# Warming matmuls, 16-bit transposes and their copies in the head of a linear attention and GeGLU kernel

## The chip, the cores and the metric

The kernel runs on one core of one Trainium2 chip. The metric is the device time of one execution in microseconds (us). The core has five engines that run side by side: TensorE (PE) for matmuls and its weight loads (PEld), VectorE (DVE), ScalarE (ACT), GpSimd (POOL) and SyncE (SP), which here only issues DMAs. Matmul results land in PSUM, which the kernel holds as one tile of eight banks of 512 f32 on each of 128 partitions (`ps_all`); DVE and ACT read them from there.

## What is computed

The reference normalises x (2048 tokens, 576 features), and adds to x a linear attention of 32 heads of 18 features and a gated feed-forward network of width 4608, both of the normalised x. Cut to what matters:

```python
xn = _layernorm(x, axis=-1)
return x + _A_ref(xn, A_wqkv, A_wo) + _B_ref(xn, B_w_gate, B_w_up, B_w_down)

def _A_ref(x, wqkv, wo):
    q, k, v = heads(x @ wqkv)
    phi = lambda t: jnp.where(t > 0, t + 1, jnp.exp(t)) + 1e-6
    kv = jnp.einsum("bhsd,bhse->bhde", phi(k), v)
    z = jnp.einsum("bhsd->bhd", phi(k))
    o = einsum(phi(q), kv) / (einsum(phi(q), z) + 1e-6)
    return o @ wo

def _B_ref(x, w_gate, w_up, w_down):
    return (_gelu(x @ w_gate) * (x @ w_up)) @ w_down
```

Inputs and output are bfloat16.

## The kernel before

**Tiles.** The 2048 tokens are 16 tiles of 128. The 576 features are cut into five chunks of contraction: four of 128 and one of 64. The last chunk is doubled: x is held 640 wide (`XW`), with a copy of the last 64 features at its end (the "twin", `x_twin`, on POOL), so that both halves of the array have something to contract. A matmul with `xn` needs it transposed, features on partitions: `xnT`, 128 x 5 x 2048.

**Pairs of row tiles.** Most matmuls use 64 of the array's 128 rows, two at a time, one on the lower (`LO`) and one on the upper (`HI`) half. A `_Unit` (L241) is such work on two PSUM banks. Its first phase, p1, runs five pairs (one per chunk), its second phase, p2, four pairs with the halves swapped between the banks; between the two POOL passes a semaphore on (the "turn", L263). All of these matmuls carry line L252. Units are K and Q (a token tile's keys or queries, 64x288 a matmul) and g (a block of the feed-forward network's gate and up products for 512 tokens, 64x512 a matmul).

**The stages.** The head runs up to about 15 us: it loads x and the first weights, normalises tiles 0 to 3 and transposes them on PE. Then come g0 to g13 (gate and up for the first 512 tokens, kept raw), mixed with K4 to K15, Q2 and Q3 (to 59 us). Tiles 4 to 15 are transposed by a DMA (`dma_transposes`, L352, issued by SP). Then follow the products of keys with xn (L566), and for each 512 tokens the remaining gate and up blocks and the down projection (L855) with the attention's output added in the same banks.

**A tile of the head, 0 to 3.** `ln_half` twice and `ln_aggr` on DVE give mean and variance; `ln_rstd` on ACT gives the reciprocal deviation by a logarithm and an exponential; `ln_norm` on DVE writes xn, in two instructions of 384 and 256 columns. `transposes` (L336) is a matmul with xn as the weights and a 64x64 identity as the moving operand, for each of the two halves of tokens and each chunk, in f32: lower half into bank 0, upper half into bank 1. Its part 0 does three chunks, part 1 two. `tp_copy` (L344, the instructions carry L347) copies part 0 of both banks with ACT and part 1 of both banks with DVE into `xnT`.

**Fillers.** `spin(NWARM)` (L227, L238) runs 35 matmuls of 128x128 zeros at the start, before any data is there, and `row_spin(5)` runs ten small ones after tile 0's transposes.

**The order.** On every engine, instructions run in the order in which they are issued. For PE that order is written out by hand (L448): t0, K0, t1, K0's second phase, K1, Q0, t2, Q1, t3, K2, K3, g0, g1 and so on, a second phase following the next unit's first. `t` stands for the transposes of a tile. For the other engines a small planner decides (`in_order`, L67): each step has an engine, a cost, a rank, predecessors and a time before which it is not due; the planner takes steps by when they can begin and, within 0.05 us, by rank. Its costs and due times (`X_AT`, `W_AT`) fix the order alone.

**Banks.** In the head K0 and Q1 use banks 4 and 5, K1 and K2 banks 6 and 7, Q0 and K3 banks 2 and 3. A unit may begin when the one before it on its banks has been copied out: for K0, Q0, K1, Q1 and K3 by a plain ACT copy (`raw`, L415), for the others through the exponential (`exp`, L420, on ACT) and two DVE steps (`clamp`, L423, and `phi`, L429). So K2 waits for K1's raw copy and K3 for Q0's. g0 and g1 use block 0 of gate and up weights, g2 and g3 block 1, g4 and g5 block 2; each block is loaded as `wr` (the last 64 features, both), `wg` and `wu` (L180 to L184).

**Loads.** SP issues, in this order, tile 0 of x, the key weights, tile 2, the query weights' main part, tile 3, the query weights' last rows, tiles 4 to 7, block 0, tiles 8 and 9, block 1, tiles 10 and 11; then it comes to the DMA transpose of tile 4, which waits for that tile's normalise, and then to block 2. Tile 1 of x is issued by ACT.

Of the kernel before, what the change touches and what calls it, by code (L numbers as in the profile page):

```python
# [8 lines left out]
ACT = mybir.ActivationFunctionType  # L9
ALU = mybir.AluOpType  # L10
BF16 = mybir.dt.bfloat16
# [3 lines left out]
P = 128  # L15
HP = 64
# [11 lines left out]
KT = 5  # L28
# [6 lines left out]
GUB = 2  # L35
NB = NF // GUB
NWBUF = 4
NWARM = 35
XW = D + HP
RAW = 14  # L40
PK0 = 18
# [45 lines left out]
def kernel(  # L87
# [11 lines left out]
    nc = tc.nc  # L99
# [14 lines left out]
    ps_all = psum.tile([P, 8, 512], F32, name="ps_all")  # L114
# [10 lines left out]
    x_sb = persist.tile([P, NS, XW], BF16, name="x_sb")  # L125
    xnT = persist.tile([P, KT, S], BF16, name="xnT")
# [4 lines left out]
    mv = persist.tile([P, NS, nc.vector.BN_AGGR_DIM], F32, name="mv")  # L131
    rstd = persist.tile([P, NS], F32, name="rstd")
    nbias = persist.tile([P, NS], F32, name="nbias")
# [18 lines left out]
    xn = apool.tile([P, NS, XW], BF16, name="xn")  # L152
# [33 lines left out]
    def load_wd(dst, f0, f1, at):  # L186
# [24 lines left out]
    ident = const.tile([P, P], BF16, name="ident")  # L211
# [7 lines left out]
        out=bm3, in_=bm3, compare_op=ALU.is_ge, fill=0.0, base=0, pattern=[[-DH, 7], [0, DH]], channel_multiplier=1,  # L219
    )  # L220
    nc.gpsimd.affine_select(
        out=bm3, in_=bm3, compare_op=ALU.is_ge, fill=0.0, base=DH - 1, pattern=[[DH, 7], [0, DH]], channel_multiplier=-1,
# [4 lines left out]
    def spin(count):  # L227

        for _ in range(count):
            nc.tensor.matmul(ps_all[:, 7, 0:P], lhsT=warm[:], rhs=warm[:], start=True, stop=True)  # L230
# [6 lines left out]

    spin(NWARM)  # L238

# [55 lines left out]
    def step(name, engine, took, rank, after, call, ready=0.0, tail=0.0):  # L295
        steps[name] = _Step(engine, took, rank, after, call, ready, tail)
# [3 lines left out]
    def ln_half(n, h):  # L300
        if n not in ln_raw:
            ln_raw[n] = asmall.tile([P, 2, nc.vector.BN_STATS_DIM], F32, name="stats")
        nc.vector.bn_stats(out=ln_raw[n][:, h, :], in_=x_sb[:, n, h * HALF:(h + 1) * HALF])  # L303

    def ln_aggr(n):
        nc.vector.bn_aggr(out=mv[:, n, :], in_=ln_raw[n][:])
# [8 lines left out]
            out=nbias[:, n:n + 1], in0=mv[:, n, 0:1], scalar1=rstd[:, n:n + 1], scalar2=-1.0, op0=ALU.mult, op1=ALU.mult,  # L315
        )

    def ln_norm(n, c0=0, c1=XW):
        if NORM[n] == "A":
            nc.scalar.activation(  # L320
                out=xn[:, n, c0:c1], in_=x_sb[:, n, c0:c1], func=ACT.Identity, bias=nbias[:, n:n + 1], scale=rstd[:, n:n + 1],
            )
        else:
            nc.vector.tensor_scalar(
                out=xn[:, n, c0:c1], in0=x_sb[:, n, c0:c1], scalar1=mv[:, n, 0:1], scalar2=rstd[:, n:n + 1],
                op0=ALU.subtract, op1=ALU.mult,
            )

    def x_twin(n, cnt):
        nc.gpsimd.tensor_copy(out=x_sb[:, n:n + cnt, D:XW], in_=x_sb[:, n:n + cnt, XW - P:D])  # L330

    HEAD = 4
    TP_CUT = 3
    TP_PARTS = ((0, TP_CUT), (TP_CUT, KT))

    def transposes(n, i):  # L336
        for kt in range(*TP_PARTS[i]):
            for b, rows in enumerate((LO, HI)):
                nc.tensor.matmul(  # L339
                    ps_all[:, b, kt * HP:(kt + 1) * HP], lhsT=xn[rows, n, kt * P:(kt + 1) * P], rhs=ident[rows, rows],  # L340
                    start=True, stop=True, skip_group_check=True,
                )

    def tp_copy(n, i):  # L344
        k0, k1 = TP_PARTS[i]
        copy = nc.vector.tensor_copy if i else nc.scalar.copy
        copy(  # L347
            out=xnT[:, k0:k1, n * P:(n + 1) * P].rearrange("p k (b t) -> p b k t", b=2),
            in_=ps_all[:, 0:2, k0 * HP:k1 * HP].rearrange("p b (k t) -> p b k t", t=HP),
        )  # L350

    def dma_transposes(n):  # L352
        nc.sync.dma_start_transpose(xnT[:, :, n * P:(n + 1) * P], xn[:, n, :])

    X_AT = [3.35, 4.40, 6.90, 9.20]
    W_AT = {"K": 6.00, "Q": 8.80}
    DMA_FREE = 12.7

# [9 lines left out]
    for n in range(NS):  # L368
        first = 1.5 * n if n < 4 else 9.0 + 3.0 * (n - 4)
        both = n // 2 * 2  # L370
        after_x = [("x", both)] if n >= 4 else []
        x_at = X_AT[n] if n < 4 else 11.5 if n < 8 else 2.1 * both
        if n < 4:
            step(("twin", n), "POOL", 0.2, first, [], lambda n=n: x_twin(n, 1), ready=x_at)
        elif n == both:
            step(("twin", n), "POOL", 0.25, first, after_x, lambda n=n: x_twin(n, 2), ready=2.6 * n)
        twin = ("twin", n if n < 4 else both)
        for h in range(2):
            step(("stats", n, h), "DVE", 0.42, first, after_x, lambda n=n, h=h: ln_half(n, h), ready=x_at)
        step(("aggr", n), "DVE", 0.16, first, [("stats", n, 0), ("stats", n, 1)], lambda n=n: ln_aggr(n), tail=0.05)  # L380
        if n < 6:
            step(("rstd", n), "ACT", 0.46, first - 2.0 * (n == 3), [("aggr", n)], lambda n=n: ln_rstd(n, 1))
        elif n == both:
            step(("rstd", n), "ACT", 0.46, first, [("aggr", n), ("aggr", n + 1)], lambda n=n: ln_rstd(n, 2))
        ready = [("rstd", n if n < 6 else both), twin]
        if NORM[n] == "A":
            step(("bias", n), "POOL", 0.27, first, ready[:1], lambda n=n: ln_bias(n))
            ready.append(("bias", n))
        on, took = ("ACT", 0.92) if NORM[n] == "A" else ("DVE", 0.45)
        if n < HEAD:  # L390
            for i, (k0, k1) in enumerate(((0, TP_CUT), (TP_CUT, KT))):
                c0, c1 = k0 * P, k1 * P
                step(("norm", n, i), on, took * (c1 - c0) / XW + 0.05, first, ready, lambda n=n, c0=c0, c1=c1: ln_norm(n, c0, c1), tail=0.05)
                step(("tp", n, i), "PE", 0.05 * (k1 - k0), 0, [("norm", n, i)] + ([("xnT", n - 1, i)] if n else []), lambda n=n, i=i: transposes(n, i), tail=0.15)
                eng = "DVE" if i else "ACT"
                step(("xnT", n, i), eng, 0.26 if i else 0.48, first, [("tp", n, i)], lambda n=n, i=i: tp_copy(n, i), tail=0.02)
            steps[("xnT", n)] = _Step("none", 0.0, first, [("xnT", n, 0), ("xnT", n, 1)], lambda: None, 0.0, 0.0)
        else:
            step(("norm", n), on, took, first, ready, lambda n=n: ln_norm(n), tail=0.05)
            load(("xnT", n), 1.25, 80, first + 2, [("norm", n)], lambda n=n: dma_transposes(n))  # L400
# [59 lines left out]
    def pe(name, took, after, call, ready=0.0):  # L460
        if name in steps:
            s = steps[name]
            s.after = s.after + ([pe_prev[0]] if pe_prev[0] else [])
        else:
            step(name, "PE", took, 0, after + ([pe_prev[0]] if pe_prev[0] else []), call, ready=ready, tail=0.17)
        pe_prev[0] = name
# [27 lines left out]
    for name in line:  # L494
        if name == ".":
            p2_step(pending.pop(0))
            continue
        kind, n = name[0], int(name[1:])
        if kind == "t":
            for i in range(2):  # L500
                pe(("tp", n, i), 0, [], None)
            if n == 0:
                pe("spin", 0.27, [], lambda: row_spin(5))
            continue
        u = _Chain()
        u.name, u.at = name, clock
        if kind in "KQ":
            u.body = _Token(kind, n, head_banks if name in HEAD_T else banks)
            b = u.body.banks
            after = [("xnT", n)]  # L510
            t1, u.t2 = 0.615, 0.49
            u.p1 = u.body.unit.rows
            u.swap = u.body.unit.swap
            u.unit_p2 = u.body.unit.p2
            at = W_AT[kind]
        else:
            u.body = _Raw(n)
            b = u.body.two
            blk = n // GUB
            after = [("xnT", m) for m in range(TPC)] + ([("gu", blk, i) for i in range(2)] if blk else [])  # L520
            t1, u.t2 = 1.08, 0.865
            u.p1 = u.body.rows
            u.swap = lambda body=u.body: body.unit.swap()
            u.unit_p2 = lambda body=u.body: body.unit.p2()
            at = 0.0 if blk else 9.1
        after += owner.get(tuple(b), [])
        pe(("p1", name), t1, after, u.p1, ready=at)
        step(("turn", name), "POOL", 0.06, clock, [("p1", name)], u.swap, tail=0.05)
        clock += t1 + u.t2
        pending.append(u)  # L530
        if len(pending) == 2:
            p2_step(pending.pop(0))
# [407 lines left out]
```

## Time and profile before

| what | value |
|---|---|
| median of three runs | 510.71 us (510.64 to 511.32) |
| the profiled execution's own time | 510.73 us |
| its span, first to last instruction | 509.0 us |
| PE busy | 503.8 us (99%), 4764 matmuls |
| DVE busy | 229.3 us (45%) |
| ACT busy | 152.2 us (30%) |
| POOL busy | 8.2 us (2%) |
| share of PE in the chain that ended last | 95% |
| chain, L252 alone | 59% of the span |
| first real matmul (tile 0's transposes) | 5.57 us |
| g0's first matmul | 15.93 us |
| raw copy of 128x576 on ACT (L415) | 0.63 us |
| normalise on DVE, 384, 256 and 640 columns | 0.37, 0.34, 0.44 us |
| transposes' copy, 384 columns on ACT, 256 on DVE | 0.48, 0.42 us |

Times are read from one profiled execution; the time around the span (510.73 less 509.0) is what the execution takes before its first and after its last instruction. A line of a timeline has start, length, engine, source line, operation, tile written and tiles read, shape, how many instructions are put together, and in brackets the engine's idle time before it and what ended that. A line of the chain that ended last has start, length and what was being done. A busy PE is not PE at its full rate: matmuls overlap, and the length of one includes what it spends in the pipeline. The profile counts a weight load (PEld) by itself.

### The profile page before, as it was taken

The page shows a single profiled execution, that of the slowest core. Times are in us where ns is not written, and L with a number is a line of the kernel's source. Part 1 is how long each engine was busy: PE and PEld are TensorE (multiplying, and loading weights), DVE is VectorE, ACT ScalarE, POOL GpSimd, SP SyncE. Part 2 cuts the span into 40 slices and gives each one's busy share as a digit, 9 for nine tenths or more (in the row PEclk, how much of TensorE's full clock was granted, in tenths as well). Part 3 has the DMA queues.
Part 4 walks back from the last instruction along what each step waited for, and adds up shares of the span by engine and source line. Part 5 has one row for each costly group of instructions (what it writes and reads, how often), then busy time and mean ns, then how long its engine had stood idle before and what let it go on. Part 6 is the DMA issues. An engine that isn't in the chain of part 4 may idle for free.

```text
span 509.0 us, 11185 instructions
## 1 busy us (share of the span) xinstructions
PE 503.8 (99%) x4764; PEld 305.5 (60%) x4764; DVE 229.3 (45%) x481; ACT 152.2 (30%) x265; POOL 8.2 (2%) x32
## 2 busy tenths in 40 slices
PE   8999999999999999999999999999999999999997
PEld 6666775445777544445777444445777444445774
DVE  5777966764101655544101655544101665544101
ACT  3888544335000433223000433233000532232000
POOL 2110000000000000000000000000000000000000
PEclk9999999999999999999999999999999999999999
DMA  9899905996200455663000455663000455640000
GB/s 262 201 229 237 295 3 157 263 259 137 71 13 13 140 152 159 168 180 107 13 13 20 140 158 148 170 175 107 12 13 25 143 152 151 175 116 14 13 12 24
DMA packets 113611, 61.58 MB, mean 121 GB/s; under 512 B 23250, under 2 KB 113562, under 8 KB 113562
## 3 DMA queue, kind: packets, MB, share of 16 engines
q1 hardware_dynamic: 113418, 60.72, 45.1%
q8 instruction: 37, 0.61, 0.5%
q10 hardware_dynamic: 144, 0.15, 0.1%
q14 instruction: 12, 0.10, 0.1%
HBM read 53.75 MB, written 2.36 MB: 110 GB/s over the span
## 4 chain that ended last, share of the span: by engine, by line
PE 95%; DVE 3%; DMA 1%; ACT 0%; issue 0%; DVEq 0%
PE ps_all L252 59%; PE ps_all L855 28%; PE ps_all L566 3%; PE ps_all L860 3%; DVE hT L429 1%; DVE z_sum L537 1%; DMA x_sb<-in_A_x_dram 1%; DVE phi_e L423 0%; PE ps_all L843 0%; PE ps_all L574 0%; DVE stats L303 0%; DVE pq L429 0%; PE ps_all L593 0%; PE ps_all L339 0%; PE ps_all L795 0%
## 5 line engine op out<-in xcount | busy, mean ns | idle before, releaser
L252 PE MATMUL ps_all<-xnT,wg 64*128 64x512 bf16 x1152 | 273.9, 376 | 0.0
L252 PE MATMUL ps_all<-xnT,wu 64*128 64x512 bf16 x1152 | 273.3, 376 | 0.0
L252 PEld LDWEIGHTS <-wg 64*128 64x128 bf16 x1152 | 108.3, 94 | 66.7
L252 PEld LDWEIGHTS <-wu 64*128 64x128 bf16 x1152 | 108.3, 94 | 65.2
L748 DVE TENSOR_TENSOR hT<-ps_all,gl 128x512 bf16<-128x512 f32 x130 | 89.8, 691 | 104.3 <-ACT gl L747 104.1
L855 PEld LDWEIGHTS <-hT 128*128 128x128 bf16 x1152 | 110.8, 98 | 30.9 <-issue 1.3
L747 ACT ACTIVATE gl<-ps_all 128x512 f32<-128x512 f32 x130 | 77.6, 597 | 164.1 <-PE ps_all L252 163.7
L869 DVE TENSOR_TENSOR res<-ps_all,x_sb 128x288 bf16<-128x288 f32 (+2 forms) x32 | 13.8, 454 | 146.3 <-PE ps_all L860 88.1
L855 PE MATMUL ps_all<-wd_a,hT 128*128 128x288 bf16 (+2 forms) x512 | 68.3, 286 | 0.0
L252 PE MATMUL ps_all<-xnT,wr 64*128 64x512 bf16 x288 | 54.9, 376 | 0.0
L855 PE MATMUL ps_all<-hT 128*128 128x288 bf16 (+2 forms) x384 | 52.4, 286 | 0.0
L769 ACT ACTIVATE gl<-ps_all 128x288 f32<-128x288 f32 x24 | 9.2, 409 | 121.4 <-PE ps_all L252 118.9
L855 PE MATMUL ps_all<-wd_m,hT 128*128 128x288 bf16 (+2 forms) x256 | 36.7, 286 | 0.0
L252 PEld LDWEIGHTS <-xnT 64*128 64x128 bf16 x576 | 30.8, 96 | 9.3 <-issue 1.0
L252 PE MATMUL ps_all<-wqkv_sb,xnT 64*128 64x288 bf16 x360 | 27.1, 295 | 0.5 <-ACT hT L415 0.2
L252 PEld LDWEIGHTS <-wr 64*128 64x128 bf16 x288 | 14.2, 94 | 16.3
L860 PE MATMUL ps_all<-m_sb,pqT 128*128 128x288 bf16 (+2 forms) x128 | 20.9, 286 | 0.0
L566 PE MATMUL ps_all<-hT,xn 128*128 128x288 bf16 x128 | 16.0, 286 | 0.0
L444 ACT CAST hT<-ps_all 128x1024 bf16<-128x1024 f32 x14 | 14.1, 1010 | 3.4 <-PE ps_all L252 3.2
L566 PEld LDWEIGHTS <-xn 128*128 128x128 bf16 x128 | 12.4, 98 | 3.5 <-issue 0.5
L860 PEld LDWEIGHTS <-pqT 128*128 128x128 bf16 x128 | 12.4, 98 | 3.3
L303 DVE BATCH_NORM_STATS2 stats<-x_sb 128x6 f32<-128x288 bf16 x32 | 12.8, 432 | 2.6 <-DMA x_sb<-in_A_x_dram 2.6
(79 smaller groups left out, 229.1 us busy)
## 6 DMA issues: line engine op xcount, KB each, us to landing
wg<-in_B_w_gate_dram SPq DMA_DIRECT2D x72, 256.0 KB, 3.0
wu<-in_B_w_up_dram SPq DMA_DIRECT2D x72, 256.0 KB, 3.6
wr<-in_B_w_gate_dram SPq DMA_DIRECT2D x36, 64.0 KB, 3.3
wr<-in_B_w_up_dram SPq DMA_DIRECT2D x36, 64.0 KB, 2.9
wd_a<-in_B_w_down_dram SPq DMA_DIRECT2D x4, 576.0 KB, 7.7
out_dram<-res SPq DMA_DIRECT2D x15, 144.0 KB, 1.8
wqkv_sb<-in_A_wqkv_dram SPq DMA_DIRECT2D x3, 576.0 KB, 5.2
x_sb<-in_A_x_dram SPq DMA_DIRECT2D x6, 288.0 KB, 4.0
```

The costliest lines, as they stand in the source:

```text
L252: return nc.tensor.matmul(self.outs[i], lhsT=self.lhs(i, rows, kt), rhs=self.rhs(i, rows, kt), start=start, stop=stop, skip_group_check=True,)
L303: nc.vector.bn_stats(out=ln_raw[n][:, h, :], in_=x_sb[:, n, h * HALF:(h + 1) * HALF])
L429: nc.vector.scalar_tensor_tensor(out=dst[:, self.n, :].rearrange("p (h c) -> p h c", h=2), in0=self.acc, scalar=0.0, in1=self.e[:].rearran ...
L444: nc.scalar.copy(out=hT[:, self.f:self.f + NF + 1:NF, :], in_=ps_all[:, self.two[0]:self.two[0] + 2, :],)
L537: nc.vector.tensor_tensor(out=(z_bf if i == NS - 1 else z_sum)[:], in0=pk[:, z_order[0], :] if i == 1 else z_sum[:], in1=pk[:, z_order[i], :],
L566: nc.tensor.matmul(ps_all[:, two[hf], :HALF], lhsT=xn[:, n, kt * P:(kt + 1) * P], rhs=pk[:, n, hf * HALF:(hf + 1) * HALF], start=(n == 0), ...
L747: nc.scalar.activation(out=gl[:], in_=ps_all[:, b[0], :], func=ACT.Gelu_apprx_tanh)
L748: nc.vector.tensor_tensor(out=hT[:, GUB * k + i, :], in0=ps_all[:, b[1], :], in1=gl[:], op=ALU.mult)
L769: nc.scalar.activation(out=e[:, :HALF], in_=acc, func=ACT.Exp)
L855: nc.tensor.matmul(self.acc(hf), lhsT=hT[:, f, j * P:(j + 1) * P], rhs=wd(f)[:, self.parts[hf]], start=(f == 0 and not paired), stop=False ...
L860: nc.tensor.matmul(self.acc(hf), lhsT=pqT[:, c, self.ts], rhs=m_sb[:, c, self.parts[hf]], start=False, stop=(paired and c == 3), skip_grou ...
L869: nc.vector.tensor_tensor(out=self.res[:, hs], in0=self.acc(hf), in1=x_sb[:, self.n, hs], op=ALU.add)
```

## The change

Five edits, all in the head.

1. `NWARM` goes from 35 to 43.
2. `ln_norm` always normalises the whole 640 columns of a tile in one instruction, in the head too.
3. `transposes` uses TensorE's transpose with a 16-bit result in place of a matmul with an f32 result, and does all five chunks in one step. The lower token half still goes to bank 0 and the upper to bank 1, now seen as bfloat16.
4. `tp_copy` copies one bank, all five chunks of one token half: ACT takes bank 0, DVE bank 1.
5. In the planner's table a head tile has one normalise and one transposing step; the transposes of a tile wait for both copies of the tile before; costs and two due times are set anew (tile 2 of x at 7.10, the second half of tile 1's statistics at 5.1).

```diff
-NWARM = 35
+NWARM = 43
...
-    def ln_norm(n, c0=0, c1=XW):
+    def ln_norm(n):
...
             nc.vector.tensor_scalar(
-                out=xn[:, n, c0:c1], in0=x_sb[:, n, c0:c1], scalar1=mv[:, n, 0:1], scalar2=rstd[:, n:n + 1],
+                out=xn[:, n, :], in0=x_sb[:, n, :], scalar1=mv[:, n, 0:1], scalar2=rstd[:, n:n + 1],
                 op0=ALU.subtract, op1=ALU.mult,
             )
...
-    TP_CUT = 3
-    TP_PARTS = ((0, TP_CUT), (TP_CUT, KT))
-
-    def transposes(n, i):
-        for kt in range(*TP_PARTS[i]):
+    def tp_bank(b):
+        return ps_all[:, b, :].bitcast(BF16).rearrange("p (k t) -> p k t", t=HP)
+
+    def transposes(n):
+        for kt in range(KT):
             for b, rows in enumerate((LO, HI)):
-                nc.tensor.matmul(
-                    ps_all[:, b, kt * HP:(kt + 1) * HP], lhsT=xn[rows, n, kt * P:(kt + 1) * P], rhs=ident[rows, rows],
-                    start=True, stop=True, skip_group_check=True,
-                )
-
-    def tp_copy(n, i):
-        k0, k1 = TP_PARTS[i]
-        copy = nc.vector.tensor_copy if i else nc.scalar.copy
-        copy(
-            out=xnT[:, k0:k1, n * P:(n + 1) * P].rearrange("p k (b t) -> p b k t", b=2),
-            in_=ps_all[:, 0:2, k0 * HP:k1 * HP].rearrange("p b (k t) -> p b k t", t=HP),
-        )
+                nc.tensor.transpose(tp_bank(b)[:, kt, :], xn[rows, n, kt * P:(kt + 1) * P], ident[rows, rows])
+
+    def tp_copy(n, b):
+        copy = nc.vector.tensor_copy if b else nc.scalar.copy
+        t0 = n * P + b * HP
+        copy(out=xnT[:, :, t0:t0 + HP], in_=tp_bank(b)[:, 0:KT, :])
...
-    X_AT = [3.35, 4.40, 6.90, 9.20]
+    X_AT = [3.35, 4.40, 7.10, 9.20]
...
-            step(("stats", n, h), "DVE", 0.42, first, after_x, lambda n=n, h=h: ln_half(n, h), ready=x_at)
+            step(("stats", n, h), "DVE", 0.42, first, after_x, lambda n=n, h=h: ln_half(n, h), ready=5.1 if (n, h) == (1, 1) else x_at)
...
-            for i, (k0, k1) in enumerate(((0, TP_CUT), (TP_CUT, KT))):
-                c0, c1 = k0 * P, k1 * P
-                step(("norm", n, i), on, took * (c1 - c0) / XW + 0.05, first, ready, lambda n=n, c0=c0, c1=c1: ln_norm(n, c0, c1), tail=0.05)
-                step(("tp", n, i), "PE", 0.05 * (k1 - k0), 0, [("norm", n, i)] + ([("xnT", n - 1, i)] if n else []), lambda n=n, i=i: transposes(n, i), tail=0.15)
-                eng = "DVE" if i else "ACT"
-                step(("xnT", n, i), eng, 0.26 if i else 0.48, first, [("tp", n, i)], lambda n=n, i=i: tp_copy(n, i), tail=0.02)
+            step(("norm", n), on, took, first, ready, lambda n=n: ln_norm(n), tail=0.05)
+            free = [("xnT", n - 1, i) for i in range(2)] if n else []
+            step(("tp", n), "PE", 0.2, 0, [("norm", n)] + free, lambda n=n: transposes(n), tail=0.15)
+            for i, copied in enumerate((0.44, 0.30)):
+                step(("xnT", n, i), "DVE" if i else "ACT", copied, first, [("tp", n)], lambda n=n, i=i: tp_copy(n, i), tail=0.02)
```

## The prediction

> **What bounds the kernel now.** I read the page first: TensorE (PE) is busy in nearly every slice, and the chain that ended last is 95% PE. So time can only be won where PE waits or runs below its rate. Listing who waited for whom, PE has four waits in the whole span: 1.1 us before the first warming matmul, 0.6 at the first transpose, 0.2 at L252 near 13.4, 0.2 near 56.5. Three lie in the first 15 us. The second view is therefore the chain in order of time:
>
> ```profile
> 13.30 0.43 DVE xnT L347
> 13.74 0.02 issue
> 13.76 0.48 ACT xnT L347
> 14.24 0.55 ACT pq L415
> 14.79 0.04 issue
> 14.83 26.96 PE ps_all L252 x306
> ```
>
> The two copies of tile 3's transposes run one after the other, then ScalarE (ACT) copies Q0 out of PSUM, and only that frees the banks of K3, which starts at 14.83. From there PE runs without a hole to 56.25. So a microsecond won ahead of g0 (its first matmul starts at 15.93) is won at the end, if the data for g0 and what follows comes as much earlier. I go by the head alone. The third view is PE's timeline from 4.5 us:
>
> ```profile
> 5.57 0.55 PE L339 MATMUL ps_all<-ident,xn 64*128 64x64 bf16 x10 [0.60 <-DVE xn L324]
> 6.68 1.38 PE L252 MATMUL ps_all<-wqkv_sb,xnT 64*128 64x288 bf16 x10
> ```
>
> The warming matmuls issue every 107 ns from 1.14 to 4.66, then PE stands idle for 0.60 us. Of L252 I then asked two stretches, 8.9 to 10.1 and 11.7 to 12.6 us:
>
> ```profile
> L252 PE MATMUL ps_all<-wqkv_sb,xnT x12: 444/444/444, 8.7 to 9.9; 64*128 64x288 bf16 x12
> L252 PE MATMUL ps_all<-wqkv_sb,xnT x16: 282/283/283, 11.7 to 12.5; 64*128 64x288 bf16 x16
> ```
>
> The same matmul takes 444 ns early and 283 ns later; pair to pair it steps by 240 and 122 ns. PE runs at half its rate until 10.5 us, where the trace's clock record begins at full rate (the clock column reads 1.00 before it too, for want of a record). The 3.9 us of matmuls from 1.05 to 4.97 did not turn the clock; 4.95 us after the work resumed at 5.57 it turned.
>
> **The copies.** Each transposed tile goes ACT first, then VectorE (DVE), or the other way round:
>
> ```profile
> 8.89 0.42 DVE L347 CAST xnT<-ps_all 128x256 bf16<-128x256 f32 x1 [0.53 <-ACT xnT L347]
> 12.34 0.48 ACT L347 CAST xnT<-ps_all 128x384 bf16<-128x384 f32 x1 [0.50 <-DVE xnT L347]
> ```
>
> Both read banks 0 and 1. Where the two engines read a bank each, at L582, they run side by side:
>
> ```profile
> 67.42 0.40 ACT L582 CAST g_sb<-ps_all 128x288 bf16<-128x288 f32 x1 [2.47 <-PE ps_all L566]
> 67.54 0.46 DVE L582 CAST g_sb<-ps_all 128x288 bf16<-128x288 f32 x1 [0.44 <-PE ps_all L566]
> ```
>
> The change gives each engine a bank, so I take its copies as side by side. ACT: 0.40 for 288 and 0.48 for 384 elements give 0.42 for 320. DVE: 0.46 for 288 f32 and 0.76 for 576 (L615) give 0.49 for 320; no row shows it reading 16 bit from PSUM, and 0.18 (L712, 64 elements, SBUF) is the lower end. I take 0.49, the nearest row; nobody waits on the difference.
>
> **The other edits.** *Eight warming matmuls*: 8 x 0.107 = 0.85 us, to 5.62, inside the idle PE time. The first transposes need the whole normalise: 5.13 + 0.45 (row of 128x640) + 0.05 = 5.63, so the cost is nothing; with tile 0 some tenths sooner it would be those tenths. *Normalise whole*: 0.45 against 0.38 for the first part, so transposes begin 0.07 later, but all ten go at once (five steps of 0.05) and the last starts at 5.83 instead of 5.87. ACT's copy did not start after the first part before either: it started at 6.15, 0.04 after the last transpose. *16-bit transposes*: no row shows one. Nearest is the same shape in f32, 0.05 a pair at half rate and 0.03 at full rate; I take that, with 0 and 0.12 (a pair of 288) as ends, 0.1 us per tile. *Second half of tile 1's stats behind tile 0's normalise* (due 5.1): 5.49 to 5.93; its rstd stood behind ACT's copy until 6.53 anyway. *Tile 1's normalise ahead of tile 2's stats*: 7.02 instead of 7.37; PE needs it at 7.86. *Added waits*: a tile's transposes wait for both copies of the tile before, which are 1 us past by then. By the planner's rule, raw K0 now stands ahead of rstd 2 on ACT: behind it wait rstd 2, then normalise 2. K0's second phase ends at 9.35, raw K0 at 10.0, rstd 2 at 10.5, normalise 2 at 10.95, and tile 2's transposes are due at 11.5: 0.5 to spare.
>
> **The sum with the clock turning at 10.5 as now.** The times of the changed kernel here and below are estimates, put together from the rows' durations, with the 0.03 to 0.05 us from one engine to the next that they show. K0 to K1 are PE-bound and stay (0.03 earlier). Tile 2's transposes end at 11.82; ACT's copy runs 11.85 to 12.27 instead of 12.34 to 12.82, raw K1 ends 12.82 instead of 13.36, and K2, which waits for those banks, starts 12.88 instead of 13.41. DVE's copy (to 12.34) and normalise 3 (to 12.65) let tile 3's transposes follow at 12.74; their copy on ACT ends 13.52, raw Q0 14.07, and K3 starts 14.12 instead of 14.83. **0.71 us.**
>
> **The sum with the clock turning early.** If 4.95 us of dense work turns it, counted from 1.05, it turns at 6.0; the lower end is 4.97 (3.9 us were not enough), the upper 10.5: 0.25 us between the last filler (6.40) and K0 stays a break. I take 6 to 7, because the idle 0.60 us is the largest break and it goes. K0's matmuls then step 122 ns for most of their length, and the order is bound by data: tile 1's transposes 7.5, K1 8.7 (DVE's copy, behind tile 2's stats, ends 8.6), Q0 9.3, tile 2's transposes 10.4, K2 11.8 (raw K1), K3 13.0 (raw Q0), and PE would be ready for g0 at 14.1. But its weights are not there:
>
> ```profile
> 9.12 0.51 SPq L184 DMA_DIRECT2D wu<-in_B_w_up_dram  x1
> wu<-in_B_w_up_dram SPq DMA_DIRECT2D x1, 256.0 KB, 5.8
> ```
>
> Issued at 9.12, landed 5.8 later: 14.90. The DMA share is about 1.1 from 5 us to there (windows of the stage), and nothing of the change moves these issues. g0's second pair needs wu and starts at 14.95 instead of 16.16. **1.2 us**, whatever more PE could do.
>
> The Trainium skill, in TensorE: Matmul & The Clock Gate, section "What's actually happening", says that the clock is set by a free-running window of 3413 ns, full rate after one busy window. The trace agrees: the record of full rate lasts 498.35 us, 146 such windows, so one ended at 7.10; by the page the clock turns there if 0.25 us of idling does not count, and the sum is again 1.2.
>
> **What is late next.** g4's wu (SP's timeline and landing):
>
> ```profile
> 15.77 1.32 SPq L353 DMA_TRANSPOSE xnT<-xn  x1
> 21.19 0.59 SPq L184 DMA_DIRECT2D wu<-in_B_w_up_dram  x1
> wu<-in_B_w_up_dram SPq DMA_DIRECT2D x1, 256.0 KB, 3.5
> ```
>
> It lands at 24.7 and g4 uses it at 25.02. SP's queue is full from 15.77, when normalise 4 (ends 15.74) lets the DMA transpose go. Normalise 4, now behind aggr 5, ends 15.22 with the late clock (0.5 earlier, plus 0.25 of slack: covers 0.71) and about 14.1 with the early one (1.6 earlier, SP free at 13.57). But the transpose cannot pass the loads ahead of it, which fill the DMA until near 16.7 (share 1.12 from 15 to 16 us, 0.32 from 16 to 17), and now its issue ends at 17.1: the gain of that queue may be only 0.4; then g4 stalls by 1.2 - 0.65 = 0.5 and 0.7 us remains. I take no stall or a small one, 0.05. K12, K13 and Q2 wait for DVE's phi with 0.05 to 0.25 us to spare, but that row of DVE work starts at 42.49 from PE's own K9 and moves with it.
>
> **Rivals.** (1) *The clock turns as before.* For it: the 0.25 us break. Against: the larger break is gone. 510.73 - 0.71 = 510.0. (2) *g4's weights give half back.* For it: the DMA is full until 16.7. Against: share 0.2 to 0.5 from 18 to 21, where the queue waits for SP. 510.0. (3) *The copies still take turns*: 510.7 with the late clock; with the early one wu still sets g0. Against it, L582. (4) *Slower: the clock turns later.* If 16-bit transposes are breaks to the clock, the dense stretch restarts after tiles 1 and 2 (8.1, 11.7) and the turn comes at 11.7 + 4.95 = 16.7. From 10.5 on PE then loses half of 6.2 us, 3.1, less 0.7: 513.1. It decides from a turn later than 10.5 + 2 x 0.7 = 11.9. Against it: filler and K matmuls on both sides, and the f32 transposes at 7.86 did not stop the turn at 10.5. The same page of the skill, Part 4, speaks for it: transpose mode does not count as busy for the clock. By its window that is one window missed, a turn at 13.9, 1.7 lost, 511.7.
>
> **How the numbers follow.** The profiled execution took 510.73, its span 509.0 with 1.7 around it, and the median of the runs is 510.71: I subtract from 510.73. Likeliest, early clock and wu in time: 510.73 - 1.2 + 0.05 = 509.6, chance 0.54. Rival 1: 0.20, rival 2: 0.10, rival 3: 0.05, rival 4: 0.09; 0.02 for wu landing sooner, down to 508.9 (PE ready at 14.1). Range 509.2 to 510.5: it holds the likeliest case, rivals 1 and 2 and the transposes' upper end (0.1 to 0.4 us above), and leaves out rivals 3 and 4. 0.2% (1.02 us) is about what a measurement of this kernel can tell from no change. Faster by more: 0.52 (the likeliest case but for 0.02 of it, and 0.02 below). Slower by more: 0.09. Within: 0.39.
>
> **What would show it.** Right: no PE idle time at 5 to 5.6; the 444 ns matmuls of L252 gone by 8 us; both L347 copies of a tile within 0.1 us of each other; PE idle ahead of g0 with DMA wu as its end, at 14.9; g4 at 23.6. Wrong: 444 ns up to 10.5 (rival 1), PE waiting for wu near 24 (rival 2), L347 after L347 (rival 3), 444 ns beyond 12 (rival 4). The DMA landing times of other executions are what I know least.

## The result and the profile after

| | before | changed |
|---|---|---|
| median (lowest to highest), 15 runs each | 510.47 us (510.21 to 511.32) | 509.52 us (509.25 to 509.92) |
| the profiled execution's own time | 510.73 us | 509.63 us |
| its span | 509.0 us | 507.8 us |
| PE busy | 503.8 us | 502.7 us |
| g0's first matmul, g0's first with wu | 15.93, 16.16 us | 14.04, 14.91 us |

The ratio of the medians is 0.998 with a 95% interval of 0.9972 to 0.9988: 0.6 to 1.4 us faster, 0.95 in the middle. The lines of the code have shifted: L344 is now the transposes' copy (L347 before), L347 the DMA transpose (L353), L408 the raw copy (L415).

PE's timeline of the changed kernel, to be read beside the two PE lines that the prediction shows:

```profile
3.70 2.11 PE L230 MATMUL ps_all<-warm 128*128 128x128 bf16 x18
5.74 0.32 PE L339 MATMUL ps_all<-ident,xn 64*128 64x64 bf16 x10
6.60 0.79 PE L252 MATMUL ps_all<-wqkv_sb,xnT 64*128 64x288 bf16 x10 [0.26 <-ACT xnT L344]
...
14.04 0.40 PE L252 MATMUL ps_all<-xnT,wr 64*128 64x512 bf16 x2
14.26 0.38 PE L252 MATMUL ps_all<-xnT,wg 64*128 64x512 bf16 x1
14.91 0.39 PE L252 MATMUL ps_all<-xnT,wu 64*128 64x512 bf16 x1 [0.27 <-DMA wu<-in_B_w_up_dram]
```

The hole at 5 us is gone, and K0's ten matmuls take 0.79 us instead of 1.38: PE runs at its full rate from the first transposes on. (In this trace the record of the full clock begins at 5.66.) The last line is a wait that the kernel before did not have. PE had started g0's first pair at 14.04 and stood until the second, which needs `wu`. The list by lines has the copies:

```profile
L344 ACT COPY xnT<-ps_all x4: 408/426/426, 6.1 to 11.9; 128x320 bf16<-128x320 bf16 x4
L344 DVE COPY xnT<-ps_all x4: 308/317/325, 6.1 to 12.1; 128x320 bf16<-128x320 bf16 x4
```

They run beside each other: ACT's begins at 10.84 and DVE's at 10.70 for tile 2, at 11.92 and 12.12 for tile 3. The chain that ended last, in order of time, has a transfer ahead of g0 where it had the two copies and ACT's copy of Q0:

```profile
9.33 0.04 issue
9.38 5.49 DMA wu<-in_B_w_up_dram
14.86 0.04 issue
14.91 25.64 PE ps_all L252 x271
```

### The profile page after: what moved, and what is told of

Same layout as the page of the kernel before. It is cut to its first block, busy times and chain, and to the rows that moved or that the text cites. A ratio compares the mean times of both kernels' runs of the same rounds, so it can differ in the third digit from the quotient of the medians.

```text
span 507.8 us, 11198 instructions
## 1 busy us (share of the span) xinstructions
PE 502.7 (99%) x4772; PEld 305.6 (60%) x4772; DVE 228.7 (45%) x477; ACT 151.9 (30%) x265; POOL 8.2 (2%) x32
## 4 chain that ended last, share of the span: by engine, by line
PE 94%; DVE 3%; DMA 2%; SPq 1%; issue 0%; ACT 0%; DVEq 0%
PE ps_all L252 58%; PE ps_all L847 28%; PE ps_all L558 3%; PE ps_all L852 3%; DVE hT L422 1%; DMA wu<-in_B_w_up_dram 1%; DMA wqkv_sb<-in_A_wqkv_dram 1%; DVE z_sum L529 1%; DVE phi_e L416 0%; PE ps_all L835 0%; PE ps_all L566 0%; DVE pq L422 0%; SPq L158 0%; PE ps_all L585 0%; PE ps_all L787 0%
## 5 line engine op out<-in xcount | busy, mean ns | idle before, releaser
L252 PE MATMUL ps_all<-xnT,wr 64*128 64x512 bf16 x288 | 57.3, 376 | 0.0
L252 PEld LDWEIGHTS <-xnT 64*128 64x128 bf16 x576 | 32.6, 94 | 6.7 <-ACT xnT L344 0.9
L437 ACT CAST hT<-ps_all 128x1024 bf16<-128x1024 f32 x14 | 14.1, 1010 | 4.0 <-PE ps_all L252 3.8
```

What stands on the lines that cost most here:

```text
L252: return nc.tensor.matmul(self.outs[i], lhsT=self.lhs(i, rows, kt), rhs=self.rhs(i, rows, kt), start=start, stop=stop, skip_group_check=True,)
L437: nc.scalar.copy(out=hT[:, self.f:self.f + NF + 1:NF, :], in_=ps_all[:, self.two[0]:self.two[0] + 2, :],)
```

## The experiments

Three questions: is it the clock that brought the gain, is it the copies, and would the 16-bit transposes slow the clock? The theories: the early clock (the prediction's likeliest case); the copies side by side; and, once the first runs had spoken, that the landing of `wu` hides what single edits do. The table has each profiled execution. "Tile 3" is the start of its first statistics on DVE; "length" runs from there to g0's first matmul. In all kernels but before, e2 and e3, DVE stands idle there until x has landed, so the length begins with the landing. In those three DVE comes from other work; in the kernel before, the tile's load was issued at 4.07 and took 4.6 us, so x had been there since 8.70 when DVE, behind its copy of tile 1, came to it:

```profile
9.23 0.20 DVE L306 BATCH_NORM_AGGREGATE mv<-stats 128x2 f32<-128x12 f32 x1
9.35 0.41 DVE L303 BATCH_NORM_STATS2 stats<-x_sb 128x6 f32<-128x288 bf16 x1
```

| kernel | tile 3 | g0 first | length | wu landed | first with wu | span |
|---|---|---|---|---|---|---|
| before | 9.35 | 15.93 | 6.58 | 14.90 | 16.16 | 509.0 |
| changed | 9.09 | 14.04 | 4.95 | 14.86 | 14.91 | 507.8 |
| changed, again (a2) | 9.75 | 14.71 | 4.96 | 15.61 | 15.66 | 508.5 |
| 35 warmings (e1) | 10.34 | 15.30 | 4.96 | 14.95 | 15.53 | 508.4 |
| before, 43 warmings (e2) | 9.12 | 15.26 | 6.14 | 14.61 | 15.49 | 508.3 |
| copies in turn (e3) | 8.89 | 14.26 | 5.37 | 14.62 | 14.67 | 507.5 |
| block 0 first (e4) | 9.12 | 14.08 | 4.96 | in time | 14.32 | 507.4 |
| block 0 first, again (e4b) | 9.06 | 14.02 | 4.96 | 14.72 | 14.77 | 509.4 |
| warming by transposes (e5) | 9.32 | 14.28 | 4.96 | 15.17 | 15.21 | 508.0 |
| no warming (e6) | 9.28 | 14.32 | 5.04 | 13.99 | 14.56 | 507.7 |
| f32 transposes (e9) | 8.93 | 14.03 | 5.10 | 14.85 | 14.89 | 507.8 |
| block 0 first, DVE order undone (x1) | 9.12 | 14.43 | 5.31 | in time | 14.66 | 507.5 |
| before, 43 warmings and DVE order (x2) | 10.26 | 16.00 | 5.74 | 14.74 | 16.24 | 509.6 |
| block 0 first, copies in turn (x3) | 9.62 | 14.81 | 5.19 | in time | 15.04 | 508.0 |

Three things are in it. The span is the second last column plus 492.8 to 493.1, but for x2 and e4b, whose weights come late again further on: what is won ahead of that matmul is won at the end. That matmul starts 0.05 us after `wu` has landed or some 0.23 after g0's first, whichever is later. And the length belongs to the kernel: it is 4.95 to 4.96 in six of the seven executions whose code of the head is that of the changed kernel but for the warming and the loads, though tile 3 comes anywhere from 9.06 to 10.34. The seventh is e6, whose clock turned late, with 5.04.

**The clock alone, and all but the eight warmings.** The first diff is e2, made in the kernel before; the second is e1, made in the changed one.

```diff
-NWARM = 35
+NWARM = 43
```

```diff
-NWARM = 43
+NWARM = 35
```

> The kernel before with 43 warming matmuls, its f32 transposes, split normalise and copies by turns kept. Theory: the clock turns before 8 us, PE would be ready for g0 at about 14.7 in spite of the copies, and the weights of g0 land at 14.9 as ever: 509.6, nearly the whole gain from this one number, with PE waiting for wu. Rival (the copies): the chain of copies is as long as before, 510.4, and g0 starts at 15.9.

> The changed kernel with 35 warming matmuls again, all else as changed. Theory (the clock gives most of the gain, and with it early g0 waits for its weights): the 0.9 us break at 4.8 to 5.7 us is back, the clock record begins between 8.9 and 12.5 us in the profile, and what is left is what the copies save with a late clock: 510.0 us (0.3 to 0.7 under the kernel before). Rival (the copies side by side gave the gain, the clock nothing): 509.5, as with 43.

e2: 510.48 us (510.00 to 511.05, 11 runs), the kernel before on the same chip 510.27 (509.93 to 511.38, 28 runs), ratio 1.0001 (0.9992 to 1.001). e1: 509.65 (509.39 to 510.18, 11 runs), ratio 0.9986 (0.9977 to 0.9995). The first K0 line of each, e2 and then e1:

```profile
6.46 0.88 PE L252 MATMUL ps_all<-wqkv_sb,xnT 64*128 64x288 bf16 x10 [0.30 <-ACT xnT L347]
```

```profile
6.49 0.79 PE L252 MATMUL ps_all<-wqkv_sb,xnT 64*128 64x288 bf16 x10 [0.29 <-ACT xnT L344]
```

Both run at the full rate. So in e2's profiled execution, with 43 warmings, the clock turned early, and the median gains nothing that it can tell. In e1's, with 35, it turned early too, against the forecast of 8.9 to 12.5: the first transposes already run at full rate, after an idle time of 0.63 us. e1 keeps most of the gain (the two intervals, of e1 and of the change, overlap widely). An early clock alone is thus not enough for the gain. e2's chain shows why; from its order of time:

```profile
10.39 0.38 DVE stats L303
...
11.03 0.30 ACT rstd L310
...
11.59 0.64 DVE xn L324 x2
...
12.63 0.43 DVE xnT L347
13.06 0.02 issue
13.09 0.48 ACT xnT L347
13.57 0.55 ACT pq L415
14.12 0.04 issue
14.16 2.85 PE ps_all L252 x36
```

With PE fast, the chain goes over DVE and ACT: tile 3's second statistics, its rstd, its normalise, one copy after the other, ACT's copy of Q0, K3. `wu` had landed at 14.61, and g0 came at 15.26.

**Copies in turn.** The changed kernel, with ACT copying three chunks of both banks and DVE two, as before:

```diff
-        t0 = n * P + b * HP
-        copy(out=xnT[:, :, t0:t0 + HP], in_=tp_bank(b)[:, 0:KT, :])
+        k0, k1 = (3, KT) if b else (0, 3)
+        two = ps_all[:, 0:2, :].bitcast(BF16).rearrange("p b (k t) -> p b k t", t=HP)
+        copy(
+            out=xnT[:, k0:k1, n * P:(n + 1) * P].rearrange("p k (b t) -> p b k t", b=2),
+            in_=two[:, :, k0:k1, :],
+        )
```

> The changed kernel with one part undone: ACT copies chunks 0 to 2 of both banks and DVE chunks 3 and 4 of both, so the two copies take turns again; 43 warming matmuls, whole normalise and 16-bit transposes stay. Theory A (the copies side by side are the gain, the earlier clock shifts nothing since the chain of copies ahead of K2 and K3 is as long with either clock): g0 starts at 15.0 to 15.3 and the time is 510.0 to 510.4, not clear of the kernel before. Theory B (early clock): 509.5, as the changed kernel.

509.43 us (509.25 to 510.51, 11 runs) beside 510.45 (35 runs), ratio 0.9983 (0.9975 to 0.9992): no loss against the change that these medians tell. DVE's timeline shows that they do take turns, and PE's that it hardly matters:

```profile
8.56 0.29 DVE L345 COPY xnT<-ps_all 128x256 bf16<-128x256 bf16 x1 [0.20 <-ACT xnT L345]
```

```profile
14.26 0.40 PE L252 MATMUL ps_all<-xnT,wr 64*128 64x512 bf16 x2
14.48 0.38 PE L252 MATMUL ps_all<-xnT,wg 64*128 64x512 bf16 x1
14.67 0.39 PE L252 MATMUL ps_all<-xnT,wu 64*128 64x512 bf16 x1
```

The length grows from 4.96 to 5.37, but g0 is still ready ahead of `wu` (14.62). The theory that the copies alone brought the gain falls, as the clock's did: in the changed kernel, either can be taken back by itself.

**f32 transposes; no warming; the changed kernel again.** e9 takes the old matmul with f32 result for the transpose, still a bank per half; e6 has no warming at the start; a2 is the changed kernel as it is.

```diff
-        return ps_all[:, b, :].bitcast(BF16).rearrange("p (k t) -> p k t", t=HP)
+        return ps_all[:, b, :].rearrange("p (k t) -> p k t", t=HP)
...
-                nc.tensor.transpose(tp_bank(b)[:, kt, :], xn[rows, n, kt * P:(kt + 1) * P], ident[rows, rows])
+                nc.tensor.matmul(
+                    tp_bank(b)[:, kt, :], lhsT=xn[rows, n, kt * P:(kt + 1) * P], rhs=ident[rows, rows],
+                    start=True, stop=True, skip_group_check=True,
+                )
```

```diff
-NWARM = 43
+NWARM = 0
```

> The changed kernel with the transposes as f32 matmuls again, still a bank per token half and a bank per engine. Both theories: DVE's copy of 320 elements takes 0.49 us instead of 0.31 to 0.33, ACT's the same 0.43; tile 1's keys and tile 3's normalise follow DVE's copy, 0.1 to 0.2 us later, which g0's wait for its weights hides: 509.5, same as the changed kernel. If the 16 bits carried part of the gain, 509.8 or more.

> The changed kernel without any warming matmul, so that the clock cannot turn before one whole window of work from 5.7 us on: 9.1 to 12.5 us. Theory A: K2 and K3 still follow the copies, g0 at 14.9 to 15.6: 509.7 to 510.2, and the difference to the changed kernel is what warming is worth at most, 0.2 to 0.7 us. Theory B: without the early clock the gain is gone, 510.3.

> The changed kernel again, for its times on the same chip as the three above and a second look at its clock. Both theories: 0.7 to 1.2 us under the kernel before, clock record from some other time between 4.4 and 7.9 us, PE waiting for g0's wu until it lands near 14.9.

All on the chip of e3. e9: 509.76 (509.30 to 510.76, 11 runs), ratio 0.9989 (0.998 to 0.9997); DVE's copy takes 0.47 instead of 0.32, PE waits for `wu` at 14.89. e6: 510.39 (509.34 to 512.20, 12 runs), ratio 1.0002 (0.999 to 1.0013). Its PE timeline:

```profile
6.52 1.38 PE L252 MATMUL ps_all<-wqkv_sb,xnT 64*128 64x288 bf16 x10
...
14.32 0.40 PE L252 MATMUL ps_all<-xnT,wr 64*128 64x512 bf16 x2
14.54 0.38 PE L252 MATMUL ps_all<-xnT,wg 64*128 64x512 bf16 x1
14.56 0.38 PE L252 MATMUL ps_all<-xnT,wu 64*128 64x512 bf16 x1
```

Here K0 was slow (the clock record begins at 8.47, earlier than the 9.1 that was forecast) and g0 lost almost nothing by it: the length is 5.04. Yet without warming the gain is gone in the median, and single executions reach 512.2. The clock may have turned still later in those; none of them was profiled, so this is not shown. a2: 510.10 (509.13 to 511.42, 11 runs), ratio 0.9994 (0.9984 to 1.0004); in its profile x came late and `wu` landed at 15.61. The same code gave 0.998 in one series and 0.9994 in another, so differences of 0.1% between the kernels here are not read from medians.

**Do transposes count as work for the clock?** In e5 the warming itself is 16-bit transposes of zeros, 39 of them:

```diff
-NWARM = 43
+NWARM = 39
-            nc.tensor.matmul(ps_all[:, 7, 0:P], lhsT=warm[:], rhs=warm[:], start=True, stop=True)
+            nc.tensor.transpose(ps_all[:, 7, :].bitcast(BF16)[:, 0:P], warm[:], ident[:])
```

> The changed kernel with its warming matmuls replaced by 39 transposes of 128x128 zeros with 16-bit result, which end at the same time (they start 0.4 us later, when the identity is there). Theory (what keeps PE going keeps the clock): the clock turns before 8 us and the time is that of the changed kernel, 509.5. Rival (transposes do not count as work for the clock): the turn comes a whole window after the last of them, 9.1 to 12.5 us, and the time is that of a late clock with the new copies, 510.0 to 510.3.

509.35 us (509.14 to 509.91, 11 runs), ratio 0.9977 (0.9969 to 0.9986). PE's timeline:

```profile
3.73 2.02 PE L230 MATMUL ps_all<-ident,warm 128*128 128x128 bf16 x17
5.68 0.45 PE L339 MATMUL ps_all<-ident,xn 64*128 64x64 bf16 x10
5.93 0.68 PE L236 MATMUL ps_all<-warm 64*128 64x128 bf16 x10
6.66 0.79 PE L252 MATMUL ps_all<-wqkv_sb,xnT 64*128 64x288 bf16 x10
```

The fillers still run at half rate (0.68; 0.44 in the changed kernel), K0 at full: the record begins at 6.45. Of the 3.4 us before it some 2.9 held nothing but transposes. In the kernel before, 0.63 us without work in such a stretch were enough for the clock not to turn at its end (the next section has this). So the transposes count. The Trainium skill, TensorE: Matmul & The Clock Gate, Part 4, says that transpose mode does not count as busy for the clock; here the run differs, and it decides.

**Block 0 first.** If `wu` hides the rest, an earlier `wu` must show it. e4 issues block 0 ahead of x's tiles 6 and 7; e4b is e4 again.

```diff
     load_x(4, 2)
-    load_x(6, 2)
     load_gu(0, 0)
     load_gu(0, 1)
+    load_x(6, 2)
```

> The changed kernel with block 0 of gate and up weights loaded ahead of tiles 6 and 7 of x. Theory (g0's weights set the end of the gain): wu lands 1.0 us sooner, at 13.9, g0 starts at 14.0 and its second pair at 14.3 instead of 14.9: 0.6 us off, 508.9. Rival (something behind g0 has no slack, g4's weights or tile 6's statistics, which now come later): the stall moves there, 509.5; or the head was never bound by wu, 509.5 as well.

> The changed kernel with block 0's weights ahead of tiles 6 and 7 of x, a second time, as the base of the two above on their chip. All theories: g0 at 14.1 without a wait for wu, 508.9 to 509.2, 1.1 to 1.4 us under the kernel before.

e4: 509.05 us (508.81 to 510.73, 6 runs), ratio 0.9974 (0.9961 to 0.9987). e4b: 509.44 (508.84 to 511.19, 11 runs), ratio 0.9983 (0.9975 to 0.9992). The first is the lowest median of the study, but neither interval is clear of the changed kernel's; the lowest times are 508.81 and 508.84 against 509.13. In e4 PE does not wait at g0:

```profile
14.08 0.40 PE L252 MATMUL ps_all<-xnT,wr 64*128 64x512 bf16 x2
14.30 0.38 PE L252 MATMUL ps_all<-xnT,wg 64*128 64x512 bf16 x1
14.32 0.38 PE L252 MATMUL ps_all<-xnT,wu 64*128 64x512 bf16 x1
```

What is late next is what the prediction's rival 2 named, g4's `wu`. The weight loads' timeline of e4 shows it, and PE's of e4b, where that block's `wu` was issued at 21.43 (19.54 in e4) and landed at 25.37:

```profile
23.43 0.09 PEld L252 LDWEIGHTS <-wu 64*128 64x128 bf16 x1 [0.38 <-DMA wu<-in_B_w_up_dram]
```

```profile
25.41 0.39 PE L252 MATMUL ps_all<-xnT,wu 64*128 64x512 bf16 x1 [1.29 <-DMA wu<-in_B_w_up_dram]
```

**The order on DVE.** Of the changed kernel's and e2's DVE timelines, the stretch around tile 3's statistics (those at 9.1 and, in e2, 10.30 are tile 3's; the normalise between is tile 2's):

```profile
9.09 0.82 DVE L303 BATCH_NORM_STATS2 stats<-x_sb 128x6 f32<-128x288 bf16 x2 [0.54 <-DMA x_sb<-in_A_x_dram]
9.83 0.43 DVE L324 TENSOR_SCALAR xn<-x_sb,mv,rstd 128x640 bf16<-128x640 bf16 x1
10.17 0.20 DVE L306 BATCH_NORM_AGGREGATE mv<-stats 128x2 f32<-128x12 f32 x1
```

```profile
9.12 0.46 DVE L303 BATCH_NORM_STATS2 stats<-x_sb 128x6 f32<-128x288 bf16 x1
9.75 0.64 DVE L324 TENSOR_SCALAR xn<-x_sb,mv,rstd 128x384 bf16<-128x384 bf16 x2 [0.16 <-ACT rstd L311]
10.30 0.45 DVE L303 BATCH_NORM_STATS2 stats<-x_sb 128x6 f32<-128x288 bf16 x1
10.78 0.21 DVE L306 BATCH_NORM_AGGREGATE mv<-stats 128x2 f32<-128x12 f32 x1
```

In the changed kernel the planner puts both halves of tile 3's statistics ahead of tile 2's normalise; tile 3's mean comes at 10.17 instead of 10.78. The diff does not state this: it follows from the planner's new table, of which no part was tried alone. x2 gives e2 that order by a rank (first diff), x1 takes it from e4 (second diff), and x3 is e4 with e3's diff.

```diff
-            step(("stats", n, h), "DVE", 0.42, first, after_x, lambda n=n, h=h: ln_half(n, h), ready=x_at)
+            step(("stats", n, h), "DVE", 0.42, first - 2.0 * (n == 3), after_x, lambda n=n, h=h: ln_half(n, h), ready=x_at)
```

```diff
-    for name in in_order(steps):
+    todo = in_order(steps)
+    todo.remove(("stats", 3, 1))
+    todo.insert(todo.index(("norm", 2)) + 1, ("stats", 3, 1))
+    for name in todo:
```

> The kernel before with 43 warming matmuls and one change of order on DVE: both halves of tile 3's statistics ahead of tile 2's normalise, as the changed kernel has them. Copies by turns, f32 transposes and split normalise stay. Theory C (with the clock early, the chain rstd 3, normalise 3, transposes 3, copy, raw Q0, K3 sets g0, and this order is what shortens it): rstd 3 starts about 0.7 us sooner (10.3 instead of 11.0), g0 at 14.6 to 14.8 instead of 15.3, then bound by its weights: 509.5 to 509.8. Theory A (the copies): g0 stays at 15.3 and the time at 510.4.

> The changed kernel with block 0's weights ahead of tiles 6 and 7 of x (so that they set nothing) and the order undone: tile 2's normalise ahead of the second half of tile 3's statistics. Theory C: aggr 3 and rstd 3 come 0.5 to 0.7 us later, g0 at 14.5 to 14.8 instead of 14.1: 509.5. Theory A: g0 stays at 14.1, 509.0.

> The changed kernel with block 0's weights ahead of tiles 6 and 7 of x and the copies by turns again. Theory C: K1 and K2 start 0.1 to 0.2 us later, g0 at 14.3: 509.2. Theory A: the copies are worth 0.5 or more once the weights do not hide them: g0 at 14.6 or later, 509.6.

Beside 510.36 (510.04 to 511.15, 33 runs): x2 510.19 (509.65 to 511.39), ratio 0.9998 (0.999 to 1.0007); x1 509.38 (509.19 to 510.94), ratio 0.9984 (0.9975 to 0.9993); x3 509.56 (509.27 to 510.94), ratio 0.9987 (0.9978 to 0.9996); 11 runs each. The medians tell neither x1 and x3 from e4b nor x2 from the kernel before; x2 misses its forecast of 509.5 to 509.8. The lengths do tell them apart: 6.14 to 5.74 with the order (x2), 4.96 to 5.31 without it (x1), 4.96 to 5.19 with copies in turn (x3). The pairs of x1 and x3 with e4 are the cleaner ones, since DVE waits for tile 3's x in all three; x2's x came 1.1 us later than e2's, when more of tile 2's work was done. The lowest times go the same way: 510.00 (e2) and 509.65 (x2), 508.84 (e4b), 509.19 (x1) and 509.27 (x3).

## Why the prediction was right, and where not

**The end: right.** g0's second pair was forecast at 14.95, held by `wu` at 14.90, and found at 14.91 and 14.86; 1.2 us were forecast for the profiled execution's span and it lost 1.2. PE ready for g0 was forecast at 14.1; it was 14.04. In the medians the gain is 0.95: the profiled 510.73, from which the prediction subtracts, is 0.26 above the median of 15 runs of the same kernel. That `wu` landed within 0.04 us of the landing in the profile before is luck. In the profiled executions of kernels with these loads it lands between 13.99 (e6) and 15.61 (a2), and a2, with the same code, has its second pair at 15.66.

**The cause: wrong in part.** The prediction hung the 1.2 on eight more warming matmuls, since "the 3.9 us of matmuls from 1.05 to 4.97 did not turn the clock". As a property of the kernel, that step failed. In e1 35 warmings did turn it, and over the profiled executions the record of full rate begins at 4.0 (e9), 4.8 (e2, e4b), 5.7 (changed, x2), 6.0 (e3), 6.2 (x1), 6.4 (x3, e5), 8.5 (e6) and 10.5 (before; a2, e1 and e4 have no such record, and run K0 at full rate). The 10.5 was one draw, not a property of 35 warmings. Nor does it take "4.95 us of dense work": the record begins 3.0 us after the first matmul in e9 and 2.9 in e6. The records of full rate of before and changed last 498.35 and 501.76 us, 3.41 apart. The Trainium skill, TensorE: Matmul & The Clock Gate, section "What's actually happening", has free-running windows of 3413 ns; the two records are 146 and 147 of them, so the runs agree, and what the prediction left out is that their phase differs between executions.

The break ahead of the first transposes does matter in some phases. Counted back from the turn in steps of 3.41 us, the last stretch ahead of it holds 0.43 us of PE idle time in e9, 0.48 in e6 and none in the others with a record. In the kernel before, the stretch from 3.69 to 7.10 holds 0.63, nearly all of it that break, and no turn came at its end; the next, without idle time, was followed by the turn at 10.52. In e1 the turn came after the last warming, issued at 4.66 and still at the slow pace, and before the first transposes at 5.60, so the stretch ahead of it held at most that break. An estimate from these numbers, if 0.48 us of idling is let pass and 0.63 is not: with 43 warmings every phase turns by 7.4, with 35 somewhat under half of them by 5.5 and the others only from 8.9 on. What that is worth in time is not shown. Some warming is worth having (e6's median); the eight more show no gain that these medians can tell (e1, e2).

**What the sum overlooked.** The early clock was made the condition that divides 1.2 from 0.71; e2 has it and is ready for g0 at 15.26, 0.65 after its `wu` has landed. So the other edits had to shorten the way from tile 3's x to g0 as well. Where DVE waits for x on both sides and one edit alone differs, the order on DVE is worth 0.35 of it (x1), the copies side by side 0.23 (x3), the 16 bits 0.14 (e9), and the warming with its earlier clock 0.08 (e6), each against 4.96. From the side of the kernel before, the table's length goes from 6.58 to 6.14 with 43 warmings and the early clock (e2), to 5.74 with the order (x2), and to 4.96 with the rest. The first of these steps is not well measured: from the landing of x, at 8.70 and 9.10, it is 1.07 instead of 0.44, and the chain that ended last in the kernel before ran over PE's slow matmuls, not over tile 3's x. Of the last step, 0.78, the copies and the 16 bits leave 0.2 to 0.4; the whole normalise and ACT's new order are in it and were not isolated. The steps need not add up, each being taken from another side. The order on DVE was no term of the prediction: it counted "tile 1's normalise ahead of tile 2's stats" and raw K0 ahead of rstd 2, and passed over tile 3's statistics. The total was right because all of them together beat `wu`, and `wu` then set the time: a limit of the right size, reached by another way than the one that was forecast.

**Sizes.** ACT's copy: 0.42 forecast, 0.43 found. DVE's: 0.49 taken, 0.32 found; from 16 bits it is faster, and 0.47 from f32 (e9). Transposes: 0.03 a pair at full rate forecast, 0.03 found (ten of them in 0.32 us, each 0.19 long). They began at 5.74 rather than 5.63. The eight warmings, put at nothing because they would be done at 5.62, are the reason: tile 0's normalise had ended at 5.53, but the last warming, issued at 5.51, ended at 5.80. With the 0.05 us from normalise to transposes that makes 0.16 us in this execution and 0.34 in a2. It did not reach g0, for the length runs from tile 3.

**The rivals.** (1), the clock as before, did not occur in the changed kernel's two profiles, and what it would have cost was not tested; the latest turn with this head, 8.47 in e6, cost 0.08 of the length. (2) did not occur in the changed kernel: the DMA transpose was issued at 13.89 instead of 15.77, and block 2's `wu` landed at 23.06 (24.74 before) and was used at 23.79. The doubt that this queue might gain "only 0.4" was unfounded here. In e4b the rival is there: PE sits idle for 1.29 us, and from g0's second pair to the end it takes 1.5 us longer than in e4. (3): that `wu` sets g0 even with copies in turn is what e3 shows; its late-clock half was not tried. (4) falls by e5. Of the signs that were named, no hole at 5 us, no 444 ns matmuls and a wait for `wu` at 14.9 held. g4's `wu` was used at 23.79 (23.6 forecast), and the copies run side by side, though their starts are 0.04 to 0.24 us apart and not all within 0.1.

**Still open:** what sets the landing of `wu` and of tile 3's x, each of which differs by more than a microsecond between executions. Where x comes late, as in e1 (10.32, with `wu` there at 14.95 and g0 at 15.30), it is x and not `wu` that sets g0. The profiled spans of the kernels with the changed head follow from the two, but for e4b's; whether the other runs' times spread for the same reason is not shown.

## What to carry to other kernels

Where several chains end at one instruction, find the one that cannot move (here a load) and ask of each edit whether its chain ends after it: taken alone, an edit then looks worthless from either side, put in alone or left out alone, though all together give the gain. Measure such edits by the length of their chain in one trace, from an event that they don't move and that the chain does wait for (the kernel before had its x 0.65 us before DVE came to it), and not by the time. And a clock's turn seen in one execution is one draw: look at others before a number of warming matmuls is fitted to it.

## What the runs showed of the hardware

- The same 43 warming matmuls turned PE to full rate anywhere between 4.0 us (e9) and 6.4 us (x3). An idle time of 0.63 us right ahead of the first transposes (e1) did not keep the rate from being full there; in the kernel before, with 0.60 us at the same place, it was half.
- The records of full rate that run through the kernel last 498.35, 501.76 or 505.17 us, 3.41 apart. Of the stretches of 3.41 us ahead of a turn the ones with most PE idle time had 0.43 (e9) and 0.48 us (e6); one with 0.63 (before) was not followed by a turn.
- 16-bit transposes count as work for that clock (e5).
- A copy of 128x320 from PSUM takes DVE 0.32 us from 16 bits and 0.47 from f32; ACT takes 0.43 from either (e9).
- The same load of 256 KB landed 5.5 us after its issue in the changed kernel's first profile and 5.85 in its second, where it was also issued 0.4 later. In e6 it took 4.6.
